# Gathering each half of an expert's list by itself, moving weight pieces out of attention's last units, and starting an expert's row preparation as soon as its rows are known

## Chip, core and metric

One core of a Trainium2 chip runs the whole program. The metric is device microseconds (us) of one execution. The engines in the profile: PE (TensorE matmul), PEld (its weight loads), DVE (VectorE), ACT (ScalarE), POOL (GpSimd), SP (SyncE, which issues most DMAs). A row with a line such as L601 names a line of the kernel before.

## What is computed

The reference chains three parts. Attention over 2 batches, 8 heads, 768 positions of 64 features: each query sees the keys less than 16 positions away and 24 block summaries (maximum of the keys, mean of the values over 32 positions). Its output, 1536 tokens of 512 features, goes through a routed layer and then a mixture:

```
# routed layer: 8 experts, each takes exactly 192 tokens
for idx in argsort(-(x @ w_gate).flatten()):   # greedy, best logit first
    tok, e = idx // 8, idx % 8
    if assigned[tok] >= 0 or counts[e] >= 192: continue
    assigned[tok] = e; counts[e] += 1
out[mask_e] = relu(x[mask_e] @ w1[e]) @ w2[e]  # 512 -> 1024 -> 512
# mixture: 4 experts, every token goes through all of them
p = domain_probs / (domain_probs.sum(-1) + 1e-9)
out = sum_e p[:, e] * (relu(x @ w1[e]) @ w2[e])
```

## The kernel before

**Numbers.** The routed layer and the mixture keep each 32-bit value as two 16-bit parts and make three matmuls for each product (`three`, L80). Each weight piece (128 x 512, 256 KB) is loaded by SP into a landing buffer (tiles `raw` and `more`, four of each after attention) and split: the high part is copied by ACT (L791), the low part is subtracted by POOL (L795), or by DVE for the first four pieces of a routed expert. `Feed` hands the pieces out in one fixed order. The first four pieces of the mixture (`POOLHI`) are split wholly by POOL.

**Attention.** 24 units of 128 tokens run in a software pipeline, `for i in range(31)`. `ORDER` and `LAST` are hand-written orders of the stages in one step. `HOOK` lists for each mixture piece handled during attention the step `i` in which it is split; the first 26 pieces (16 of mixture expert 0, 10 of expert 1) are listed, the last four at steps 27 and 28. Router steps `r0` to `r9` (`Router.first`) run in the same pipeline; their DVE lines are L520 to L545.

**Router.** `Router.phases` is a generator. Each of its 8 phases `p` fills one expert: it finds the tokens that go to it (DVE chains with small PE matmuls between, lines L622 to L706), turns the list into indices (`so`, L710; 24 to 36 matmuls into `pi`, L722), and gathers the token rows with two indirect DMAs from POOL (`gather`, L910 to L920). Each phase's 192 tokens stand in two lists of 128 and 64, since tiles hold 128 rows. A `yield r` says how long the code before it is thought to take, and the code behind it is put into the instruction stream only after about that much other work.

**The planner.** All of this is ordered while the program is written out, by a clock of the planner's own: `clock[0]` counts the matmul work put into the stream so far, in us; `clock[1]` is when the router's next step may be put in:

```
clock[1] = max(clock[:2]) + SLOW[min(known[0] + 1, len(SLOW) - 1)] * r + HOP
```

with `SLOW` 1.0 (1.3 from expert 4 on) and `HOP` 0.3. The work comes in units: of `mixture(t0, nt)`, which handles `nt` = 1, 2 or 3 tiles of 128 tokens and yields after each unit (0.66, 1.3 or 1.95 us of matmuls), and of the routed experts' jobs: one `start` (waits for the list, transposes the gathered rows on PE, splits them into `xeh` on ACT and `xel` on DVE), four `up` and four `down` (2.0 us each). `PLAN` says which experts run beside which mixture call, from when on (`at`) and how far apart (`gap`). What is left of the jobs when a mixture call ends is put in one after another (the drain, `while jobs`). `start` may be put in when `steady()` holds: its list is known, 7 us of the planner's clock have gone by (`LATE`), and its first four weight pieces have been handed out. A drained `start` does not ask `steady()`.

Of the kernel before, what the change touches and what calls it, by code (L numbers as in the profile page):

```python
# [10 lines left out]
F32 = mybir.dt.float32  # L11
F16 = mybir.dt.float16
BF = mybir.dt.bfloat16
I32 = mybir.dt.int32
# [28 lines left out]
class Feed:  # L43
# [16 lines left out]
    def next(self, free):  # L60

        self.pump()
        if self.used in self.held and self.clock[0] >= self.since[self.used] + 3.0 and free(self.used):
            self.jobs[self.used][1](self.held.pop(self.used))
            self.used += 1
            self.pump()
# [24 lines left out]
        (6, 3, [6, 7], 2.5, 4.1), (9, 3, [], 0.0, 1.0)]  # L91
WB = 5
FEED = [0.96, 0.71, 365.54]
HOOK = [10, 13, 15, 17, 18, 18, 19, 19, 20, 20, 21, 21, 22, 22, 23, 23, 24, 24, 25, 25, 26, 26, 27, 27, 28, 28]

NEXT = 4
SCHED = {"prep": [1, 1, 2, 2, 3, 4, 4, 5], "sum": 8, "v": 9, "store": 10, "spread": 11, "kq0": 4, "kq1": 7, "vn": 6}
# [362 lines left out]
class Router:  # L460
# [152 lines left out]
    def phases(self, ps, wrk, filled, place, gather, free):  # L613

        nc, m, oh, ohb, lm, E, NCH = self.nc, self.m, self.oh, self.ohb, self.lm, self.E, self.NCH
        over_chunks, over_experts = self.over_chunks, self.over_experts
        SC = NCH // 3
        four, top = self.four, self.top16
        for p in range(E):
            last = p == E - 1  # L620
            if p:
                nc.vector.tensor_tensor(lm, self.L, over_chunks(self.pen), op=OP.add)  # L622
                nc.vector.tensor_reduce(m[:, 0], lm, axis=AX.X, op=OP.max)
                if not last:

                    nc.vector.max(top[:, 0, :8], m[:, 0])
                    nc.vector.match_replace(top[:, 1, :NCH], top[:, 0, :8], m[:, 0], -3e38)
                    nc.vector.max(top[:, 0, 8:], top[:, 1, :NCH])
                    yield 1.2
                nc.vector.tensor_tensor(lm, lm, over_experts(m[:, 0]), op=OP.is_equal)  # L630
                nc.vector.tensor_tensor(lm, lm, over_chunks(self.wt), op=OP.mult)
                nc.vector.tensor_reduce(m[:, 1], lm, axis=AX.X, op=OP.max)
                nc.vector.tensor_tensor(oh, lm, over_experts(m[:, 1]), op=OP.is_equal)
                nc.vector.tensor_tensor(ohb, oh, over_experts(self.alive), op=OP.mult)
                if last:
                    yield 1.2
            new = ohb
            if p and not last:

                s4 = top[:, 0].rearrange("x (a b) -> x a b", b=4)  # L640
                yield from self.beyond(ps, wrk, s4[:, :3, 3], four[:, 5, :1])
                nc.vector.scalar_tensor_tensor(four[:, :4], self.n4.unsqueeze(1).to_broadcast([128, 4, 4]),
                                               four[:, 5, :1], s4.rearrange("x a b -> x b a"),
                                               op0=OP.is_equal, op1=OP.mult)
                cand = four[:, 6]
                nc.vector.tensor_reduce(cand, four[:, :4], axis=AX.X, op=OP.add)
                yield 1.4
                yield from self.beyond(ps, wrk, cand[:, :3], four[:, 5, 1:2])
                nc.vector.scalar_tensor_tensor(four[:, 7], self.n4, four[:, 5, 1:2], cand,
                                               op0=OP.is_equal, op1=OP.mult)  # L650
                nc.vector.tensor_reduce(four[:, 5, 2:3], four[:, 7], axis=AX.X, op=OP.add)
                yield 1.4
                pm = ps.tile([128, 128], F32, name="rt", bufs=2)
                nc.tensor.transpose(pm, four[:, 5, 2:3].to_broadcast([128, 128]), self.identf)
                yield 0.6

                nc.vector.tensor_reduce(four[:, 5, 3:4], pm, axis=AX.X, op=OP.max)
                nc.vector.tensor_scalar(m[:, 1], m[:, 0], four[:, 5, 3:4], None, op0=OP.is_gt)
                nc.vector.tensor_scalar(m[:, 2], m[:, 0], four[:, 5, 3:4], None, op0=OP.is_equal)
                new = wrk.tile([128, NCH, E], BF, name="new", bufs=1)  # L660
                nc.vector.tensor_tensor(oh, ohb, over_experts(m[:, 2]), op=OP.mult)
                nc.vector.tensor_tensor(lm, ohb, over_experts(m[:, 1]), op=OP.mult)
                above = wrk.tile([128, E], BF, name="above", bufs=1)
                nc.vector.tensor_reduce(four[:, :2].rearrange("x a b -> x (a b)"), lm.rearrange("x c e -> x e c"),
                                        axis=AX.X, op=OP.add)
                nc.vector.tensor_copy(above, four[:, :2].rearrange("x a b -> x (a b)"))
                yield 2.6
                pc = ps.tile([128, NCH, E], F32, name="rt", bufs=2)
                nc.tensor.matmul(pc, self.ones, over_chunks(above), start=True, stop=False, skip_group_check=True)
                self.ahead(pc, oh)  # L670
                yield 0.8
                nc.vector.tensor_tensor(lm, pc, over_chunks(self.remx), op=OP.is_lt)
                lead, tied = m[:, 1], m[:, 2]
                room = self.col
                nc.vector.tensor_reduce(room, lm, axis=AX.X, op=OP.min)
                nc.vector.tensor_tensor(room, room, tied, op=OP.mult)
                nc.vector.tensor_tensor(lead, lead, room, op=OP.add)
            elif not last:
                new = wrk.tile([128, NCH, E], BF, name="new", bufs=1)
                nc.vector.tensor_reduce(m[:, 1], lm, axis=AX.X, op=OP.min)  # L680
            if not last:
                nc.vector.tensor_tensor(new, ohb if p else oh, over_experts(m[:, 1]), op=OP.mult)
                yield 2.0
            pt = ps.tile([128, NCH, E], F32, name="rt", bufs=2)
            nc.tensor.matmul(pt, self.ones, new, start=True, stop=True)
            asg = self.asg if p else new
# [21 lines left out]
            so = [wrk.tile([128, SC, self.cap], F16, name="so", tag="g", bufs=GB) for _ in range(NCH // SC)]  # L708
# [5 lines left out]
                    yield 1.0  # L714
            while not free(p):
                yield 0.0
            pi = ps.tile([128, 2], F32, name="rt", bufs=2)

            for n, half, q0, s0 in sorted(((n, half, q0, s0) for half in range(2) for t, p0, n, s0 in (place(p, half),)
                                           for q0 in {0, p0}), reverse=True):  # L720
                for c in range(NCH):
                    nc.tensor.matmul(pi[q0:q0 + n, half:half + 1], so[c // SC][:, c % SC, s0:s0 + n],  # L722
                                     self.tok[:, c:c + 1], start=(c == 0 and n == 128), stop=(c == NCH - 1),
                                     skip_group_check=True)
            if p:
                yield 0.9
            gather(p, pi)
            if not p:
                nc.vector.tensor_copy(self.asg, new)
            if not last:  # L730
# [10 lines left out]
def attention_moe_mixture_kernel(  # L741
# [13 lines left out]
    nc = tc.nc  # L755
    NTOK, DM = out.shape
    E = moe_w_gate.shape[1]
    ND, _, F = moe2_w1.shape
    KD, KF = DM // 128, F // 128
    CAP = NTOK // E  # L760
    ROW = DM + ND
# [8 lines left out]
    xd = tc.dram_tile([NTOK, ROW], F32, name="xd")  # L770
# [128 lines left out]
    def place(p, half):  # L899

        t = 3 * (p // 2)
        if p % 2 == 0:
            return ((t, 0, 128, 0), (t + 1, 0, 64, 128))[half]
        return ((t + 1, 64, 64, 0), (t + 2, 0, 128, 64))[half]
# [2 lines left out]
    PD = mcst.tile([128, NST, ND], F32, name="pd")  # L907
    XG = {}

    def gather(p, pi):  # L910
        idx = []
        for half in range(2):
            t, p0, n, s0 = place(p, half)
            idx.append(wrk.tile([128, 1], I32, name="idx", bufs=4))
            nc.vector.tensor_copy(idx[half][:n], pi[:n, half:half + 1])
        for half in range(2):
            t, p0, n, s0 = place(p, half)
            nc.vector.tensor_copy(IDS[p0:p0 + n, t:t + 1], pi[p0:p0 + n, half:half + 1])
            XG[p, half] = wrk.tile([128, ROW], F32, name="xg", bufs=2)
            nc.gpsimd.indirect_dma_start(out=XG[p, half][p0:p0 + n], out_offset=None, in_=xd[:, :],  # L920
                                         in_offset=bass.IndirectOffsetOnAxis(ap=idx[half][:n, :1], axis=0))

    taken = set()
    route = router.phases(ps, wrk, filled, place, gather, lambda p: p < 1 or p - 1 in taken)
# [160 lines left out]
    for t0, nt, side, at, gap in PLAN:  # L1085
        jobs = [job for p in side for job in expert(p)]

        def begin():

            n = next((n for n, (f, _) in enumerate(jobs) if f.__name__ == "start"), 0)  # L1090
            if 0 < n <= 4 and jobs[n][1]():
                jobs.pop(n)[0]()

        now = 0.0
        for us in mixture(t0, nt):
            now += us
            spend(us)
            begin()
            while jobs and now >= at and jobs[0][1]():
                jobs.pop(0)[0]()  # L1100
                spend(2.0)
                at = max(at + gap, now)
        while jobs:
            begin()
            jobs.pop(0)[0]()
            spend(2.0)
# [27 lines left out]
```

## Time and profile before

| | us |
|---|---|
| median of 3 runs | 870.28 |
| range of the runs | 869.6 to 871.71 |
| the profiled execution, its own time | 871.12 |
| its span in the trace | 869.3 |
| PE busy | 790.5 (91% of the span) |
| DVE, ACT, POOL busy | 456.6, 291.1, 248.9 |

Between the span and the execution's own time lie 1.82 us outside the trace. Attention's pipeline ends near 136 us; from about 150 us on PE works on routed experts and mixture. A bracket at the end of a timeline row is the time for which the engine stood idle before the instruction and what ended it.

### The profile page before, as it was taken

How to read it: one execution, taken by the hardware profiler on the slowest of the kernel's cores; microseconds unless marked ns; L12 is line 12 of the kernel's file. 1: busy time of each engine (PE TensorE's matmuls, PEld its weight loads, DVE VectorE, ACT ScalarE, POOL GpSimd, SP SyncE). 2: the span in 40 equal slices, each digit the busy share in tenths (PEclk: the TensorE clock that was granted, in tenths of full speed). 3: DMA queues.
4: the chain of work that ended last, by engine and by line, in shares of the span. 5: the costliest groups of instructions: out<-in, count | busy, mean ns of one | idle time of the engine just before them, and what ended most of it. 6: DMA issues, size and time to landing. Idle time of an engine off the chain costs nothing.

```text
span 869.3 us, 17212 instructions
## 1 busy us (share of the span) xinstructions
PE 790.5 (91%) x6782; PEld 545.7 (63%) x6822; DVE 456.6 (53%) x1153; ACT 291.1 (33%) x668; POOL 248.9 (29%) x260
## 2 busy tenths in 40 slices
PE   5888974988889998989989999997999999999997
PEld 4777753866786577685556565764666664554553
DVE  6349698678765765556474566656333121321121
ACT  5788874653431222241131121412332310110110
POOL 6344553886340222160011130512412300000001
PEclk9999995999999999999999999999999999999999
DMA  9989664874412402230330121223332000000000
GB/s 199 194 207 221 176 177 141 241 221 138 128 34 80 120 16 77 69 93 2 98 104 13 33 79 55 86 77 101 94 95 61 1 1 25 13 1 1 1 1 37
DMA packets 111537, 76.27 MB, mean 88 GB/s; under 512 B 25441, under 2 KB 98273, under 8 KB 111073
## 3 DMA queue, kind: packets, MB, share of 16 engines
q1 hardware_dynamic: 109472, 68.86, 30.3%
q0 software_dynamic: 1984, 6.32, 2.4%
q8 instruction: 53, 0.87, 0.4%
q14 instruction: 28, 0.22, 0.1%
HBM read 68.77 MB, written 6.42 MB: 86 GB/s over the span
## 4 chain that ended last, share of the span: by engine, by line
PE 71%; DVE 17%; ACT 4%; DMA 4%; issue 3%; POOL 1%; SPq 0%; POOLq 0%; ACTq 0%; DVEq 0%
PE mm L80 38%; PE po L80 25%; DVE g L601 2%; DMA kq<-in_k_dram 2%; PE sc L309 1%; DVE so L710 1%; DVE hml L949 1%; DVE wp L795 1%; DVE ga L539 1%; ACT kt L263 1%; PE ta L329 1%; PE rt L595 1%; PE rt L722 1%; PE po L345 1%; ACT qt L263 1%
## 5 line engine op out<-in xcount | busy, mean ns | idle before, releaser
L948 ACT ACTIVATE hmh<-mm 128x384 f16<-128x384 f32 (+2 forms) x160 | 68.2, 426 | 308.5 <-PE mm L80 302.0
L80 PEld LDWEIGHTS <-wp 128*128 128x128 f16 (+1 forms) x1536 | 133.1, 101 | 18.6 <-issue 11.6
L949 DVE SCALAR_TENSOR_TENSOR hml<-mm,hmh 128x384 f16<-128x384 f32 (+2 forms) x160 | 75.3, 475 | 126.0 <-ACT hmh L948 125.7
L80 PEld LDWEIGHTS <-hmh 128*128 128x128 f16 x768 | 73.6, 99 | 78.9 <-issue 1.3
L795 POOL TENSOR_TENSOR wp<-raw,wp 128x512 bf16<-128x512 f32 x56 | 67.7, 1230 | 133.6 <-ACT wp L791 132.2
L601 DVE TENSOR_SCALAR g<-rt,m 128x384 bf16<-128x384 f32 x144 | 80.4, 608 | 0.7 <-PE rt L586 0.7
L80 PE MATMUL mm<-xeh,wp 128*128 128x192 f16 x512 | 74.2, 258 | 3.4 <-ACT xeh L952 3.2
L80 PE MATMUL mm<-xel,wp 128*128 128x192 f16 x256 | 66.0, 258 | 8.3 <-DVE xel L953 8.3
L1051 POOL DMA_INDIRECT out_dram<-acc,ids x12 | 12.2, 1018 | 204.0 <-DVE acc L1035 184.1
L795 POOL TENSOR_TENSOR wp<-more,wp 128x512 bf16<-128x512 f32 x40 | 45.4, 1156 | 84.2 <-ACT wp L791 84.2
L80 PE MATMUL mm<-heh,wp 128*128 128x192 f16 x512 | 69.5, 249 | 0.0
L80 PEld LDWEIGHTS <-hml 128*128 128x128 f16 x384 | 37.8, 98 | 46.4 <-issue 1.4
L80 PE MATMUL mm<-hel,wp 128*128 128x192 f16 x256 | 63.8, 249 | 0.0
L1035 DVE SCALAR_TENSOR_TENSOR acc<-po,pn,acc 128x512 f32<-128x512 f32 x36 | 25.7, 745 | 55.7 <-PE po L80 55.6
L80 PEld LDWEIGHTS <-w2k 128*128 128x128 f16 (+1 forms) x480 | 42.4, 98 | 19.2
L949 DVE SCALAR_TENSOR_TENSOR hel<-mm,heh 128x384 f16<-128x384 f32 x32 | 17.8, 558 | 63.1 <-ACT heh L948 63.0
L920 POOL DMA_INDIRECT xg<-xd,idx x16 | 16.1, 1003 | 122.0 <-DVE m L731 99.2
L948 ACT ACTIVATE heh<-mm 128x384 f16<-128x384 f32 x32 | 15.7, 491 | 88.6 <-PE mm L80 88.6
L80 PEld LDWEIGHTS <-w23dt.float 128*128 128x128 f16 x320 | 29.5, 98 | 14.4 <-issue 1.3
L80 PEld LDWEIGHTS <-w21dt.float 128*128 128x128 f16 x320 | 30.0, 99 | 12.6
L791 ACT ACTIVATE wp<-more 128x512 f16<-128x512 f32 x64 | 37.0, 622 | 1.3 <-DMA more<-in_moe_w_dram 1.1
L80 PE MATMUL po<-w23dt.float,hml 128*128 128x512 f16 x96 | 36.9, 384 | 0.6 <-issue 0.2
(255 smaller groups left out, 1926.5 us busy)
## 6 DMA issues: line engine op xcount, KB each, us to landing
raw<-in_moe_w_dram SPq DMA_DIRECT2D x110, 256.0 KB, 3.5
more<-in_moe_w_dram SPq DMA_DIRECT2D x82, 256.0 KB
vb<-in_v_dram SPq DMA_DIRECT2D x16, 240.0 KB, 6.0
kq<-in_k_dram SPq DMA_DIRECT2D x8, 384.0 KB, 6.5
kq<-in_q_dram SPq DMA_DIRECT2D x8, 384.0 KB, 5.9
vn<-in_v_dram SPq DMA_DIRECT2D x4, 768.0 KB, 9.9
xd<-x SPq DMA_DIRECT2D x48, 64.0 KB, 4.0
vb<-vsum_d SPq DMA_DIRECT2D x4, 292.5 KB
```

What stands on the lines that cost most here:

```text
L80: nc.tensor.matmul(o, a[i], b[j], start=first and n == 0, stop=last and n == 2, skip_group_check=True)
L263: nc.scalar.activation(o[:, :, :, :, r], pt[r * 64:r * 64 + 64].rearrange("x j (c i) -> x c i j", i=R), AF.Copy, scale=scale)
L309: nc.tensor.matmul(sc[:, t, p], QT[Q][:, p, 2 * ch + t], KT[Q][:, p, 2 * ch + t], start=False, stop=True, skip_group_check=True)
L329: nc.tensor.transpose(pt[:KC, p], AE[u][:, p], identf)
L601: nc.vector.tensor_scalar(g[:, c - c0], row, m[:, 0, c:c + 1], None, op0=OP.is_le)
L791: nc.scalar.activation(hi, r, AF.Copy)
L795: (eng or nc.gpsimd).tensor_tensor(lo, r, hi, op=OP.subtract)
L920: nc.gpsimd.indirect_dma_start(out=XG[p, half][p0:p0 + n], out_offset=None, in_=xd[:, :], in_offset=bass.IndirectOffsetOnAxis(ap=idx[half] ...
L948: nc.scalar.activation(h[0], p, AF.Relu)
L949: nc.vector.scalar_tensor_tensor(h[1], p, 0.0, h[0], op0=OP.max, op1=OP.subtract)
L1035: nc.vector.scalar_tensor_tensor(acc[i], po[i], s, acc[i], op0=OP.mult, op1=OP.add)
L1051: nc.gpsimd.indirect_dma_start(out=out[:, :], out_offset=bass.IndirectOffsetOnAxis(ap=IDS[:, t0 + i:t0 + i + 1], axis=0), in_=acc[i], in_o ...
```

## The change

1. `HOOK` has 24 entries in place of 26. Steps 12 and 16 get one piece more, steps 27 and 28 lose two each. Pieces 8 and 9 of mixture expert 1 are now among the four handled between attention and the routed experts, and four instead of two of that expert's pieces come behind the 16 of the first routed expert.
2. Four of the router's `yield`s are longer.
3. The matmuls for an expert's list go into one PSUM tile for each half, and `gather` handles one half. In phase 0 the first half's gather is put in ahead of the second half's matmuls; in the other phases both gathers follow the matmuls, the longer half first.
4. `begin()` also puts in a `start` that is the first of the jobs (`n == 0`), without waiting for `at`, and then the next job is held back 2.5 us of the planner's clock.

```diff
-HOOK = [10, 13, 15, 17, 18, 18, 19, 19, 20, 20, 21, 21, 22, 22, 23, 23, 24, 24, 25, 25, 26, 26, 27, 27, 28, 28]
+HOOK = [10, 12, 13, 15, 16, 17, 18, 18, 19, 19, 20, 20, 21, 21, 22, 22, 23, 23, 24, 24, 25, 25, 26, 26]
...
                 if last:
-                    yield 1.2
+                    yield 2.6
...
                 nc.vector.tensor_reduce(four[:, 5, 2:3], four[:, 7], axis=AX.X, op=OP.add)
-                yield 1.4
+                yield 2.0
                 pm = ps.tile([128, 128], F32, name="rt", bufs=2)
...
                 nc.vector.tensor_copy(above, four[:, :2].rearrange("x a b -> x (a b)"))
-                yield 2.6
+                yield 3.6
                 pc = ps.tile([128, NCH, E], F32, name="rt", bufs=2)
...
                 nc.vector.tensor_tensor(new, ohb if p else oh, over_experts(m[:, 1]), op=OP.mult)
-                yield 2.0
+                yield 2.8
             pt = ps.tile([128, NCH, E], F32, name="rt", bufs=2)
...
-            pi = ps.tile([128, 2], F32, name="rt", bufs=2)
...
+            todo = []
+            for half in sorted(range(2), key=lambda half: -place(p, half)[2]):
+                t, p0, n, s0 = place(p, half)
+                pi = ps.tile([128, 1], F32, name="rt", bufs=2)
+                for q0 in sorted({0, p0}, reverse=True):
+                    for c in range(NCH):
+                        nc.tensor.matmul(pi[q0:q0 + n], so[c // SC][:, c % SC, s0:s0 + n],
+                                         self.tok[:, c:c + 1], start=(c == 0), stop=(c == NCH - 1),
+                                         skip_group_check=True)
+                todo.append((half, pi))
+                if not p:
+                    gather(p, *todo.pop())
             if p:
                 yield 0.9
-            gather(p, pi)
+            for half, pi in todo:
+                gather(p, half, pi)
...
+    def gather(p, half, pi):
+        t, p0, n, s0 = place(p, half)
+        idx = wrk.tile([128, 1], I32, name="idx", bufs=4)
+        nc.vector.tensor_copy(idx[:n], pi[:n])
+        XG[p, half] = wrk.tile([128, ROW], F32, name="xg", bufs=2)
+        nc.gpsimd.indirect_dma_start(out=XG[p, half][p0:p0 + n], out_offset=None, in_=xd[:, :],
+                                     in_offset=bass.IndirectOffsetOnAxis(ap=idx[:n, :1], axis=0))
+        nc.vector.tensor_copy(IDS[p0:p0 + n, t:t + 1], pi[p0:p0 + n])
...
-            n = next((n for n, (f, _) in enumerate(jobs) if f.__name__ == "start"), 0)
-            if 0 < n <= 4 and jobs[n][1]():
+            n = next((n for n, (f, _) in enumerate(jobs) if f.__name__ == "start"), 9)
+            if n <= 4 and jobs[n][1]():
                 jobs.pop(n)[0]()
+                return n == 0
...
-            begin()
+            if begin():
+                at = max(at, now + 2.5)
```

## Rows read from the trace of the kernel before

**Rows 1.** The page's chain of work that ended last, shares by engine.
```profile
PE 71%; DVE 17%; ACT 4%; DMA 4%; issue 3%; POOL 1%; SPq 0%; POOLq 0%; ACTq 0%; DVEq 0%
```

**Rows 2.** Windows: length, busy us (count) of PE, PEld, DVE, ACT, POOL; clock, DMA, GB/s.
```profile
157.00:625.00 468.00, 433.94 (x3995) 309.30 (x4020) 291.58 (x763) 136.42 (x304) 150.68 (x133) 0.98 0.31 88
...
180.00:200.00 20.00, 14.72 (x158) 10.06 (x157) 16.66 (x28) 8.79 (x22) 17.13 (x16) 0.91 0.67 203
```

**Rows 3.** Waits of PE, 157 to 625 us: total us, times, longest.
```profile
PE mm L80 <- DVE xel L953: 7.9, 6, 3.0
PE mm L80 <- ACT xeh L952: 2.7, 6, 0.8
```

**Rows 4.** Timeline of PE: start us, duration, instruction, idle before and its releaser.
```profile
192.05 0.32 PE L654 MATMUL rt<-identf,four 128*128 128x128 f32 x1 [3.62 <-DVE four L651]
200.28 0.22 PE L669 MATMUL rt<-above,ones 128*128 128x96 bf16 x1 [1.72 <-DVE above L666]
216.21 1.00 PE L722 MATMUL rt<-tok,so 128*128 128x1 f16 x28 [0.72 <-DVE so L710]
230.40 0.32 PE L80 MATMUL mm<-xel,wp 128*128 128x192 f16 x1 [1.53 <-DVE xel L953]
334.90 0.20 PE L685 MATMUL rt<-new,ones 128*128 128x96 bf16 x1 [1.16 <-DVE new L682]
347.14 1.00 PE L722 MATMUL rt<-tok,so 128*128 128x1 f16 x28 [1.23 <-DVE so L710]
373.68 0.32 PE L80 MATMUL mm<-xel,wp 128*128 128x192 f16 x1 [3.04 <-DVE xel L953]
444.93 0.32 PE L80 MATMUL mm<-xel,wp 128*128 128x192 f16 x1 [1.58 <-DVE xel L953]
566.67 0.20 PE L669 MATMUL rt<-above,ones 128*128 128x96 bf16 x1 [2.40 <-DVE above L666]
596.94 0.22 PE L685 MATMUL rt<-ohb,ones 128*128 128x96 bf16 x1 [3.30 <-DVE ohb L634]
```

**Rows 5.** Windows of two stretches behind such waits.
```profile
444.00:450.00 6.00, 5.08 (x39) 4.33 (x39) 2.88 (x8) 1.42 (x3) 0.33 (x1) 0.72 0.04 11
566.00:572.00 6.00, 5.33 (x53) 5.16 (x53) 2.09 (x7) 0.33 (x1) 1.70 (x2) 0.72 0.00 0
```

**Rows 6.** Timelines of DVE and POOL in attention's last steps.
```profile
128.00 0.23 DVE L522 SCALAR_TENSOR_TENSOR lm<-L,m,wt 128x8 f32<-128x8 f32 x1
128.45 0.23 DVE L526 TENSOR_SCALAR oh<-lm,m 128x8 bf16<-128x8 f32 x1
...
131.20 0.77 DVE L522 SCALAR_TENSOR_TENSOR lm<-L,m,wt 128x8 f32<-128x8 f32 x1
...
132.20 0.89 DVE L526 TENSOR_SCALAR oh<-lm,m 128x8 bf16<-128x8 f32 x1
...
130.79 2.27 POOL L795 TENSOR_TENSOR w21dt.bfloat<-raw,w21dt.float 128x512 bf16<-128x512 f32 x2 [3.92 <-ACT w21dt.float L791]
```

**Rows 7.** Timelines of DVE and POOL at the first gather.
```profile
143.47 0.22 DVE L915 CAST idx<-rt 128x1 int32<-128x1 f32 x2 [1.09 <-PE rt L722]
...
149.91 0.69 DVE L953 SCALAR_TENSOR_TENSOR xel<-mm,xeh 128x512 f16<-128x512 f32 x1 [0.35 <-ACT xeh L952]
...
144.50 1.18 POOL L920 DMA_INDIRECT xg<-xd,idx  x1 [7.24 <-ACT wp L791]
```

**Rows 8.** Later gathers: tile `xg`'s landing times, POOL's timeline; ACT's and DVE's behind a `down`.
```profile
DMA to landing us min/median/max: 2.8/3.4/4.9
...
219.63 0.91 POOL L920 DMA_INDIRECT xg<-xd,idx  x1 [6.88 <-DVE idx L915]
220.84 0.97 POOL L920 DMA_INDIRECT xg<-xd,idx  x1 [0.30 <-DVE hml L949]
...
366.08 0.33 ACT L952 ACTIVATE y1h<-mm 128x192 f16<-128x192 f32 x1 [8.86 <-PE mm L80]
...
366.44 0.36 DVE L953 SCALAR_TENSOR_TENSOR y1l<-mm,y1h 128x192 f16<-128x192 f32 x1 [2.81 <-ACT y1h L952]
```

More of the change, by code (lines that the diff above doesn't have):

```diff
@@ L716, in phases @@
                 yield 0.0
-            pi = ps.tile([128, 2], F32, name="rt", bufs=2)
[L719 to L724, printed above, removed]
+            todo = []
[10 more added lines that the diff above has]
+                    gather(p, *todo.pop())
             if p:
                 yield 0.9
-            gather(p, pi)
+            for half, pi in todo:
+                gather(p, half, pi)
             if not p:
@@ L908, in attention_moe_mixture_kernel @@
     XG = {}
[L910 to L921, printed above, removed]
+    def gather(p, half, pi):
[6 more added lines that the diff above has]
+        nc.vector.tensor_copy(IDS[p0:p0 + n, t:t + 1], pi[p0:p0 + n])
     taken = set()
```

## The prediction

> **What bounds the kernel now.** I read the chain of waits first. PE holds 71% of it and DVE 17% [rows 1]: behind attention the time is matmul work plus the moments in which PE waits. None of the matmuls of that work is removed or added, so the change can only move those moments and attention's end. The windows give their size: from 157 to 625 us PE was busy 433.94 of 468 us, so it idled 34 us, at a mean clock of 0.98 [rows 2]. Next the waits of PE in that stretch. Two kinds are to be seen. In the first, a new expert's first `up` matmuls wait for its rows' two parts: 7.9 us for `xel` and 2.7 for `xeh`, six times each [rows 3], 10.6 us. In the second, one of the router's small matmuls stands in PE's queue and its DVE operand is late: 3.62, 1.72, 0.72, 1.16, 1.23, 2.40 and 3.30 us in the timeline [rows 4]. PE works in order, so all matmuls behind such a one wait too. Third, the clock behind some of these waits: from 444 to 450 and from 566 to 572 us the mean granted clock is 0.72 [rows 5]. With levels of 1.2 and 2.4 GHz that loses 0.28 x 6 = 1.7 us each. Such dips stand behind six of the waits (192.05, 230.40, 347.14, 373.68, 444.93, 566.67); the 3.30 us at 596.94 has none.
>
> I make the sum against the profiled execution, 871.12 us, which is 0.84 above the median.
>
> **Attention's end.** Four pieces stood in steps 27 and 28. Around the first low parts that POOL makes of them (2.27 us from 130.79), DVE's L522 takes 0.77 us against 0.23 before it, and L526 0.89 against 0.23 [rows 6]: 0.54 + 0.66 = 1.2 us of DVE, whose chain ends attention. With no piece there I count that as removed. Steps 12 and 16 get one piece each, where PE, ACT and DVE share the chain; between nothing and the same 1.2 us I take 0.4, since there the load is spread over more engines. Net -0.8, bounds -1.2 to 0.
>
> **First gather.** `idx` of both halves is copied at 143.47, after DVE waited 1.09 us for the matmuls of both; POOL starts the first gather at 144.50 [rows 7]. With one half done first, its copies fall into that wait: DVE is through 0.4 us earlier (two index casts and two copies, half of them moved). The gather itself starts up to 1.4 us earlier, but before `xel` at 149.91 DVE had stood idle only 0.35 us, so what came next was DVE, not the rows. I take -0.4; bounds -1.4 and 0.
>
> **Longer yields.** What matters is how many units of work lie between a DVE step and the small matmul that reads it. A step of 1.4 + 0.3 (HOP) fills with three units of 0.66, 1.98 us; 2.0 + 0.3 with four, 2.64. Phase 1 at 192.05: 0.66 of 3.62 goes. In the same way, at 200.28, 2.9 against 3.9 gives 5 or 7 units of 0.65, so 1.3 of 1.72 goes. At 334.90 (2.3 against 3.1, two or three units of 1.3) all 1.16. At 566.67 the factor 1.3 makes 3.68 or 4.98, two or three units of 1.95; less a job's 2.0 for a unit, 1.83 of 2.40. At 596.94, 1.86 or 3.68, one or two units: 1.94 of 3.30. Sum 6.9 [rows 4], and the dip behind 566.67, 1.7 [rows 5]: -8.6. Below this: nothing, if DVE's delay is carried on to the next step.
>
> **Starts put in early.** The planner, followed unit by unit, puts two units between `start` and the first `up` for experts 2, 4 and 6, where before the `up` followed at once. `xel` waits of experts 1, 3 and 4 are 1.53, 3.04 and 1.58 [rows 4]; what is left of 7.9 is 1.75 for experts 2, 5 and 6, 0.58 each, and with 2.7 / 6 = 0.45 for `xeh` [rows 3] a plain start costs 1.03. So experts 2 and 6 save 1.03 each and expert 4 saves 2.03 and its dip of 1.7 [rows 5]: -5.8. Expert 1's start stays in a drain, but the router is a step behind and no comparison of its search stands ahead of `xel` on DVE; I take its wait from 1.98 to 1.03, and half of the dip: -1.8, bounds -2.7 to +1. Expert 5's stays at 1.03.
>
> **Phase 3's list.** At 347.14 the index matmuls waited 1.23 us for `so` [rows 4] with one unit of 1.3 between; now this lies in the drain with jobs of 2.0 between. The wait and its dip go: -2.9, bounds -2.9 to 0.
>
> **The price: expert 3's start.** Each router phase is now up to 2.4 us longer (0.6 + 1.0 + 0.8), and whole units round it up. Phase 3's gather moves from 163.2 to 177.5 on the planner's clock, and expert 3's `start`, which is drained and asks nothing, stands right there; before it stood 16 us behind. So nothing covers the gather. Behind the last `down` of expert 2: 0.33 + 0.36 us for its parts, on the queue of which the index casts stand [rows 8], about 0.4 for the casts and POOL's reaction, 1.21 until POOL issues the second gather (219.63 to 220.84), which is the half that `start` reads first, and 3.4 to its landing [rows 8]: 5.7, and a plain start's 1.03, 6.7 us of idle PE. It replaces 3.04 + 0.45 = 3.5; the dip stays. +3.2, bounds +1.5 (landing 2.8, less queue) to +8 (landing 4.9, and DVE as crowded as at 373.68).
>
> **Given back elsewhere.** In phase 1 two `so` steps now have 1.31 us between where 1.95 stood, behind which 0.72 was waited [rows 4]: +1.3, and a dip of 1.7, as the 1.23 at 347.14 has one. And the two pieces that left attention are split again about 200 us, where POOL is busy 17.13 of 20 us and PE idles most [rows 2]; two more low parts of 1.14 us (half of 2.27 [rows 6]) stretch DVE by up to 2.3 us, some of it in front of PE: +1.0. Together +4.0, bounds +1 to +6.
>
> On that last term the Trainium skill (SBUF — State Buffer, Who interferes with whom) speaks against the change: VectorE and GpSimd share a port pair as a lock, and whichever starts first keeps it for the whole instruction while the other is blocked. The rows of attention's end agree in kind: DVE lost 1.2 us of the 2.27 that POOL worked. By the rule taken to its full length the term would be 2.3 and not 1.0, and the sum 1.3 us higher; the split of DVE's waiting that the rows show is what I use.
>
> **Sum.** -0.8 - 0.4 - 8.6 - 5.8 - 1.8 - 2.9 + 3.2 + 4.0 = -13.1: 858.0 for the profiled execution, 857.2 for the median. I say 857.
>
> **Rivals.** (a) *The idle goes, the clock does not come back.* Dips stand behind waits of 1.23 as of 3.62 us, and 3.30 had none [rows 4], so which waits bring one is not plain. With the dips of 1.7, 1.7, 0.85 and 1.7 kept, 6.0 is lost again: 863. (b) *The wait only moves.* DVE's router chain is as long as before, and POOL still stretches it; if each longer gap is used up by DVE being further behind at the next small matmul, the yields' 8.6 and phase 3's 2.9 are gone: 857.2 + 11.5 = 868.7, no change that can be told. For it: 3.62 us for a single operand at 192.05. Against it: at most router matmuls PE did not wait at all. (c) *The other side: rows that come too late at drained starts.* Expert 1's gather to start shrinks too, from 7.2 to 5.85 us of planner's clock, about what the chain above needs (5.7). If landings take 4.9 us [rows 8] and DVE is crowded as at 373.68 (3.04), each idles about 10.5: 4.9 in place of 3.4, and 3.0 in place of 0.58 more, with their own dips. Expert 3 then costs 4 more than counted, and expert 1 gives back its 1.8 and loses 8.5 and 0.9. That is 15 us: 872. It is slower than before from about 16 us on, which a third such start, expert 5's, would bring (+9): 881.
>
> **How the numbers follow.** A measurement of this kernel can tell about 0.3%, 2.6 us, from no change. Chances: the forecast, 847 to 862, 0.52; (a), 860 to 866, 0.22; (b), and other losses that leave about the old time, 0.15; (c) 0.11. (a) and the forecast lie below 867.7, (b) between 867.7 and 872.9 in most of its cases, (c) on either side of 872.9, mostly above. Faster 0.76, same 0.13, slower 0.11. The range reaches from 847, where the bounds of the gains come out (0.4 more at attention's end, 1.0 at the gather, 0.9 at expert 1, 1.7 at expert 3, 3 given back less, together 7 and the uneven rest 3), to 869, which takes in (b).
>
> **What would show it.** Right: the rows of L654, L669, L685 with idle times of about 3.0, 0.4 or less, 0.6, 1.4 and none; no waits for `xel` at experts 2, 4 and 6; a window of 0.72 at neither expert 4's first `up` nor phase 6's L669; one wait of 6 to 7 us for `xg` and `xeh` at expert 3; attention's last DVE steps about 1 us earlier; from 157 us on PE idle of some 24 in place of 34 us. Wrong: idle at L672's and L722's neighbours grown by what left the others (b), dips of the same number as before (a), or PE standing at `xg` at expert 1 (c).

## The result and the profile after

The changed kernel takes 855.75 us (median of 4 runs, 853.86 to 856.93) against 869.94 for the kernel before beside it; ratio 0.9837, 95% interval 0.9806 to 0.9867. The forecast was 857. The profiled execution took 856.93 us, 14.2 less than the one before; its span is 855.2 us, 14.1 less.

The page's chain of waits, which answers to [rows 1]: DVE's share fell from 17 to 12%, that of DMA rose from 4 to 6.

```profile
PE 73%; DVE 12%; DMA 6%; ACT 4%; issue 3%; POOL 2%; SPq 0%; POOLq 0%; DVEq 0%; ACTq 0%
```

The windows of [rows 2]. PE idles 23.4 us of 468, where it idled 34.1 (32.4 in a second execution of the kernel before, whose trace holds 4036 matmuls in this window and not 3995, so a part of the 34.1 may be missing records). The mean clock is 0.98 as before.

```profile
157.00:625.00 468.00, 444.56 (x4020) 311.24 (x4019) 289.63 (x755) 136.14 (x302) 143.89 (x126) 0.98 0.30 86
180.00:200.00 20.00, 16.25 (x171) 10.50 (x169) 16.90 (x29) 8.55 (x21) 17.80 (x17) 0.91 0.70 209
```

PE's waits from 157 to 625 us, total, times, longest [rows 3]. The router's L654, L669 and L685, five of the waits in [rows 4], are not among them any more. New at the top is PE waiting for gathered rows, and second the mixture's own matmuls waiting for `hml` (the low part of relu, on DVE; 7.1 us, where 0.5 us stood before).

```profile
PE mm L972 <- DMA xg<-xd,idx: 8.4, 2, 7.6
PE mm L80 <- DVE hml L951: 7.1, 6, 3.8
PE mm L80 <- DVE xel L955: 2.9, 3, 2.1
PE mm L80 <- ACT xeh L954: 2.6, 3, 1.2
PE rt L595 <- DVE g L601: 1.3, 4, 0.4
```

PE's timeline at those waits. The first two stand where L654 and L669 of phase 1 waited 3.62 and 1.72; then expert 1's start, expert 2's, expert 3's (7.64, the price), and expert 5's.

```profile
192.06 0.22 PE L80 MATMUL mm<-y0h,w21dt.float 128*128 128x128 f16 x1 [3.75 <-DVE hml L951]
205.37 0.22 PE L80 MATMUL mm<-y0h,w2k 128*128 128x128 f16 x1 [1.09 <-DVE hml L951]
...
227.25 1.05 PE L972 MATMUL mm<-identf,xg 64*128 64x64 f32 x8 [0.80 <-DMA xg<-xd,idx]
228.98 0.24 PE L80 MATMUL mm<-xeh,wp 128*128 128x192 f16 x1 [0.69 <-ACT xeh L954]
229.70 0.24 PE L80 MATMUL mm<-xel,wp 128*128 128x192 f16 x1 [0.48 <-DVE xel L955]
...
300.57 1.04 PE L972 MATMUL mm<-identf,xg 128*128 128x128 f32 x8 [0.35 <-DVE hml L951]
302.28 0.27 PE L80 MATMUL mm<-y0h,w2k 128*128 128x256 f16 x1 [0.67 <-DVE hml L951]
...
367.17 1.74 PE L972 MATMUL mm<-identf,xg 64*128 64x64 f32 x8 [7.64 <-DMA xg<-xd,idx]
369.59 0.32 PE L80 MATMUL mm<-xeh,wp 128*128 128x192 f16 x1 [0.68 <-ACT xeh L954]
370.32 0.32 PE L80 MATMUL mm<-xel,wp 128*128 128x192 f16 x1 [0.41 <-DVE xel L955]
...
541.17 0.24 PE L80 MATMUL mm<-xeh,wp 128*128 128x192 f16 x1 [1.23 <-ACT xeh L954]
543.46 0.24 PE L80 MATMUL mm<-xel,wp 128*128 128x192 f16 x1 [2.05 <-DVE xel L955]
```

What is late at 192.05 and 192.06 is one small DVE operation, the same in both kernels. L649 handles 4 elements a partition and takes 0.22 us at its shortest; here it takes 4.13 us before and 4.16 after. `hml` is the next but one behind it on DVE. Beside it POOL splits weights without a break, and L649 ends when that row of splits ends: at 191.71 against 191.69 us before, at 191.62 against 191.60 after, and within 0.03 us in all fourteen traces below. The operations just ahead of it, L609 to L611, ran in the same stretch and took 0.16 to 0.18 us. The first four lines are of before, the others of the changed kernel.

```profile
187.39 0.16 DVE L611 TENSOR_REDUCE four<-four 128x1 f32<-128x3 f32 x1
187.58 4.13 DVE L649 SCALAR_TENSOR_TENSOR four<-n,four 128x4 f32<-128x4 f32 x1
188.31 1.16 POOL L795 TENSOR_TENSOR w2k<-more,w2v 128x512 bf16<-128x512 f32 x1
189.42 2.27 POOL L795 TENSOR_TENSOR w23dt.bfloat<-more,w23dt.float 128x512 bf16<-128x512 f32 x2
...
187.46 4.16 DVE L649 SCALAR_TENSOR_TENSOR four<-n,four 128x4 f32<-128x4 f32 x1
191.65 0.16 DVE L651 TENSOR_REDUCE four<-four 128x1 f32<-128x4 f32 x1
191.72 0.68 DVE L951 SCALAR_TENSOR_TENSOR hml<-mm,hmh 128x128 f16<-128x128 f32 x3
...
185.98 4.51 POOL L801 TENSOR_TENSOR w2k<-raw,w2v 128x512 bf16<-128x512 f32 x4
190.43 1.17 POOL L801 TENSOR_TENSOR w2k<-more,w2v 128x512 bf16<-128x512 f32 x1
```

Expert 3's start on POOL, in the order in which the prediction followed it. The second gather is issued 1.29 us behind the first, and its rows arrive when PE goes on at 367.17, 5.25 us after issue; the median counted with was 3.4 [rows 8]. In the window around it the mean clock is 0.53 for 11 us.

```profile
360.63 0.98 POOL L921 DMA_INDIRECT xg<-xd,idx  x1 [3.56 <-DVE idx L919]
361.92 0.97 POOL L921 DMA_INDIRECT xg<-xd,idx  x1 [0.30 <-DVE remx L742]
...
363.00:374.00 11.00, 5.74 (x34) 4.87 (x35) 4.23 (x12) 1.50 (x3) 1.15 (x1) 0.53 0.55 148
```

DVE at attention's end [rows 6]. L522 and L526 take 0.23 us, as forecast, with no piece beside them. But L534 and L539 now stand 0.53 and 0.29 us waiting for ACT and PE, so L539 starts 1.86 us behind L522 where it started 2.06 us behind it before (133.26 - 131.20; first line, of before).

```profile
133.26 1.14 DVE L539 TENSOR_SCALAR ga<-rows,m 128x768 bf16<-128x768 f32 x2
...
131.98 0.23 DVE L522 SCALAR_TENSOR_TENSOR lm<-L,m,wt 128x8 f32<-128x8 f32 x1
...
132.44 0.23 DVE L526 TENSOR_SCALAR oh<-lm,m 128x8 bf16<-128x8 f32 x1
133.20 0.35 DVE L534 SCALAR_TENSOR_TENSOR ge<-rows,m,before 128x128 bf16<-128x128 f32 x1 [0.53 <-ACT rows L530]
133.84 1.15 DVE L539 TENSOR_SCALAR ga<-rows,m 128x768 bf16<-128x768 f32 x2 [0.29 <-PE cnt L564]
```

**A finer measure.** Attention's end moves between executions; what follows it much less. So I also compare, in each trace, the time from the first matmul of expert 0's `up` (L80, `mm<-xeh`; 150.33 us before, 150.00 after) to the end of the span. All times in us; "L710 starts" is the first comparison that builds the index matrices, the mark of attention's end. e1 to e4 were taken on one chip and e5 to e10, c1 and c2 on another; each ratio is against the kernel before on the same chip.

| trace | L710 starts | first up | first up to end | ratio of the runs (95%) |
|---|---|---|---|---|
| before | 139.7 | 150.33 | 719.0 | |
| before, again (c1) | 138.9 | 149.45 | 717.2 | |
| changed | 140.0 | 150.00 | 705.2 | 0.9837 (0.9806 to 0.9867) |
| changed, again (c2) | 140.2 | 150.11 | 705.5 | |
| e1, yields alone | 142.5 | 153.10 | 705.5 | 0.9896 (0.9868 to 0.9924) |
| e2, starts alone | 140.0 | 150.57 | 707.2 | 0.9883 (0.9863 to 0.9903) |
| e3, HOOK alone | 137.8 | 148.44 | 721.4 | 1.0042 (1.0015 to 1.0069) |
| e4, gather alone | 137.5 | 147.48 | 719.9 | 1.0008 (0.9982 to 1.0034) |
| e5, changed, old yields in phases 1 to 3 | 139.2 | 149.47 | 704.8 | 0.9867 (0.9813 to 0.9921) |
| e6, changed, old HOOK | 136.3 | 146.31 | 700.4 | 0.9833 (0.9793 to 0.9874) |
| e7, both of these | 137.7 | 147.62 | 704.7 | 0.9807 (0.9762 to 0.9853) |
| e8, e7 with starts ahead of the weights | 136.6 | 146.62 | 695.1 | 0.9726 (0.9679 to 0.9774) |
| e9, e8 with L669's longer yield in phase 1 | 137.8 | 147.78 | 696.9 | 0.9719 (0.9642 to 0.9797) |
| e10, e8 with all longer yields | 142.9 | 152.74 | 706.5 | 0.9854 (0.9772 to 0.9935) |

### The profile page after: what moved, and what is told of

It reads as the page before. It is cut to its first block, busy times and chain, and to the rows that moved or that the text cites. A ratio compares the mean times of both kernels' runs of the same rounds, so it can differ in the third digit from the quotient of the medians.

```text
span 855.2 us, 17243 instructions
## 1 busy us (share of the span) xinstructions
PE 787.2 (92%) x6822; PEld 542.9 (63%) x6822; DVE 456.9 (53%) x1153; ACT 291.8 (34%) x668; POOL 250.3 (29%) x260
## 4 chain that ended last, share of the span: by engine, by line
PE 73%; DVE 12%; DMA 6%; ACT 4%; issue 3%; POOL 2%; SPq 0%; POOLq 0%; DVEq 0%; ACTq 0%
PE mm L80 40%; PE po L80 27%; DVE g L601 2%; DMA xd<-x 2%; DMA kq<-in_k_dram 1%; DMA xg<-xd,idx 1%; ACT kt L263 1%; PE rt L595 1%; POOL w20dt.bfloat L801 1%; PE rt L724 1%; ACT qt L263 1%; DVE hml L951 1%; DVE so L710 1%; DVE ga L539 1%; DMA vsum_d<-vs 1%
## 5 line engine op out<-in xcount | busy, mean ns | idle before, releaser
L80 PEld LDWEIGHTS <-wp 128*128 128x128 f16 (+1 forms) x1536 | 132.0, 101 | 14.6 <-issue 7.2
L80 PEld LDWEIGHTS <-hmh 128*128 128x128 f16 x768 | 73.3, 98 | 79.0 <-issue 0.8
L801 POOL TENSOR_TENSOR wp<-raw,wp 128x512 bf16<-128x512 f32 x54 | 65.8, 1238 | 132.6 <-ACT wp L797 132.5
L601 DVE TENSOR_SCALAR g<-rt,m 128x384 bf16<-128x384 f32 x144 | 80.5, 609 | 0.0
L80 PE MATMUL mm<-xeh,wp 128*128 128x192 f16 x512 | 75.3, 260 | 3.1 <-ACT xeh L954 3.1
L801 POOL TENSOR_TENSOR wp<-more,wp 128x512 bf16<-128x512 f32 x42 | 48.1, 1166 | 74.4 <-ACT wp L797 74.2
L80 PE MATMUL mm<-xel,wp 128*128 128x192 f16 x256 | 66.5, 260 | 3.4 <-DVE xel L955 3.4
L80 PE MATMUL mm<-heh,wp 128*128 128x192 f16 x512 | 68.0, 246 | 0.0
L80 PEld LDWEIGHTS <-hml 128*128 128x128 f16 x384 | 37.7, 98 | 45.8 <-issue 0.8
L80 PE MATMUL mm<-hel,wp 128*128 128x192 f16 x256 | 63.0, 246 | 0.2 <-DVE hel L951 0.2
L80 PEld LDWEIGHTS <-w2k 128*128 128x128 f16 (+1 forms) x480 | 42.5, 98 | 21.1 <-issue 1.9
L80 PEld LDWEIGHTS <-w21dt.float 128*128 128x128 f16 x320 | 29.4, 98 | 16.8 <-issue 3.9
L80 PEld LDWEIGHTS <-w23dt.float 128*128 128x128 f16 x320 | 29.6, 98 | 14.0 <-issue 1.3
L797 ACT ACTIVATE wp<-raw 128x512 f16<-128x512 f32 x64 | 37.1, 621 | 1.7 <-DMA raw<-in_moe_w_dram 1.7
```

The lines of the kernel that those rows point to most:

```text
L80: nc.tensor.matmul(o, a[i], b[j], start=first and n == 0, stop=last and n == 2, skip_group_check=True)
L601: nc.vector.tensor_scalar(g[:, c - c0], row, m[:, 0, c:c + 1], None, op0=OP.is_le)
L797: nc.scalar.activation(hi, r, AF.Copy)
L801: (eng or nc.gpsimd).tensor_tensor(lo, r, hi, op=OP.subtract)
```

## The experiments

**Each part alone, on the kernel before.** e1 has the four `yield`s of the diff, e2 the new `begin()` with its `at = max(at, now + 2.5)`, e3 the new `HOOK`, e4 the two hunks of `pi` and `gather`; nothing else differs.

> The four longer yields alone, on the kernel before. The theory (each part by its own step of the sum): the waits of PE at L654, L669 and L685 go (about 9 us with a clock dip), but expert 3's start comes to stand 2 us of planner's clock behind its gather instead of 16, which costs about 5 us there; ratio 0.993 to 0.998. The rival (the wait only moves: DVE is as late at the next step): 0.998 to 1.003, with the same PE idle from 155 to 625 us as before, about 34 us.

Measured: 0.9896, a gain of 1.0% where the theory gave 0.2 to 0.7%, and 705.5 us from the first up. No wait of 0.5 us is left at L669 and L685, and PE idles 23.8 us from 155 to 625 us, so the rival falls as an account of the whole. At L654 it holds: the wait is now one of 3.75 us for `hml`. Expert 3's start waits 2.62 us for `xg` and 1.05 for DVE, as expected in kind, but with its parts that is 4.4 us where 3.8 stood, not 5 more. Expert 5's start, which the theory did not name, waits 3.8 us where 0.9 stood.

> The new begin() alone. The theory: two units of the mixture now lie between start and first up of experts 2, 4 and 6, so their waits for xel and xeh go and so does the clock dip at expert 4: about -6 us, 0.993 (0.990 to 0.996). The rival (the starts' gain hangs on the longer yields, since without them DVE's search comparisons still stand ahead of xel): 0.998 or more.

Measured: 0.9883, and 707.2 us. Expert 4's waits are gone, expert 6's are down to 0.87 us for `hml`, as the theory says. It is more than the theory gave: the waits at 334.90, 347.14, 566.67 and 596.94 of [rows 4], which the prediction gave to the yields and to phase 3's list, are gone here too, with the old yields. That the jobs now fall elsewhere among the router's steps is the likely reason; no run tests it. The rival falls.

> HOOK alone. The theory after seeing the changed kernel: DVE's work at attention's end is shorter, but the steps there then wait for ACT and PE, and the step's earlier units lose as much: attention's end within 0.7 us of before, 0.998 to 1.002. The rival, as the prediction had it: 0.8 us earlier at attention's end, 1 us lost again at 200 us, also no difference in the time, but the index comparisons (L710) would begin about 0.8 us earlier.

Measured: 1.0042, slower by 0.4%, with the interval above 1. L710 starts at 137.8 in this trace, but that says little: over the fourteen traces above it starts at 139.0 on average in the ten with the old list (136.3 to 142.9) and at 139.3 in the four with the new one (137.8 to 140.2). The difference from both traces of the kernel before is behind the first up: 721.4 us against 719.0 and 717.2. The index matmuls of phase 1 wait longer, 1.58 us where 0.72 was [rows 4], and a dip stands behind that wait:

```profile
215.18 0.97 PE L722 MATMUL rt<-tok,so 128*128 128x1 f16 x27 [1.58 <-DVE so L710]
...
216.00:221.00 5.00, 5.00 (x65) 4.99 (x63) 1.94 (x14) 1.21 (x5) 1.51 (x2) 0.66 0.33 88
```

That the part costs time is shown by the runs. Where it costs it is seen in this one trace: 0.9 us of the wait and 1.7 us of the dip, and single dips come and go between executions (last section). Its benefit at attention's end is not shown; the rival's earlier end is not borne out over the traces.

> The gather by halves alone. The theory: the first gather starts about 0.4 us earlier, DVE is the engine that the first up waits for, so the first up begins 0.3 to 0.7 us earlier and nothing else changes: 0.9985 to 1.0005. The rival (POOL is held by something else than the index cast): no earlier start of the first gather.

Measured: 1.0008, no difference. From the start of L710 to the first up are 10.0 us (147.48 - 137.48) against 10.65 before (150.33 - 139.68): 0.65 us earlier, near the upper end of the theory. This repeats best of all: 10.6 to 10.65 us in the five traces with the old gather, 9.9 to 10.3 in the nine with the new one. The theory's reason does not hold; PE's wait ahead of the first up is for the rows (First gather, below).

**Undoing parts of the changed kernel.** e5 keeps the old yields in phases 1 to 3, e6 the old `HOOK`, e7 both.

```diff
-                yield 2.0
+                yield 2.0 if p > 3 else 1.4
                 pm = ps.tile([128, 128], F32, name="rt", bufs=2)
...
-                yield 3.6
+                yield 3.6 if p > 3 else 2.6
                 pc = ps.tile([128, NCH, E], F32, name="rt", bufs=2)
...
-                yield 2.8
+                yield 2.8 if p > 3 else 2.0
             pt = ps.tile([128, NCH, E], F32, name="rt", bufs=2)
```

> The changed kernel, with the old yields in phases 1 to 3 and the new ones from phase 4 on (and in the last). Expert 3's gather then stands 9.9 us of planner's clock ahead of its start again instead of directly before it. The theory: the 7.6 us wait for xg goes, and the time from the first up to the end falls from 705.2 to about 699 us (696 to 702); phases 1 and 3 get waits of about 1 us back. The rival (the longer yields earn their gain in phases 1 to 3, and the wait for xg only takes the place of other waits): 705 us or more from the first up to the end.

Measured: 704.8 us, no gain; the theory falls and the rival holds. The wait for `xg` is gone, but expert 3's start still waits 1.24 + 2.04 us for its parts, and phase 1's waits are back:

```profile
199.31 0.22 PE L669 MATMUL rt<-above,ones 128*128 128x96 bf16 x1 [1.91 <-DVE above L666]
216.31 0.84 PE L724 MATMUL rt<-tok,so 128*128 128x1 f16 x23 [1.58 <-DVE so L710]
```

> The changed kernel with the old HOOK. The theory: the two pieces behind attention cost about 2.4 us around 200 us (as HOOK alone showed) and buy nothing measurable at attention's end, so from the first up to the end 702 to 704 us against 705.2. The rival (with the other parts in, the pieces fit where PE no longer waits): 705 us, no difference.

Measured: 700.4 us from the first up, 5 us less than the changed kernel. Expert 1's start waits as long as in the changed kernel (0.76 + 0.69 + 0.48 = 1.93 us against 1.97). What is gone is the wait of 0.77 us for `hml` at 215.58, 0.8 us of the wait for `xg` (6.87) and the dip behind expert 1's start, 1.7 us: three stretches run at the lower clock instead of four. The direction is the theory's, in one trace; the ratios of the runs (0.9833 against 0.9837) don't tell the two apart.

> Both of these: old HOOK, and the old yields in phases 1 to 3. The theory: both savings, 695 to 700 us from the first up to the end, ratio to the kernel before 0.974 to 0.982. The rival (each saving only moves a wait): 703 us or more.

Measured: 704.7 us, 0.9807. The two savings do not add; the rival holds.

**A version that beats both.** e8 takes e7 and lets a start go ahead without its weights.

```diff
             need(p)
-            ready(p, 3)
+            if p == 0:
+                ready(p, 3)
...
-            return known[0] >= p and clock[0] >= when[p] + LATE and feed.used > feed.at["p", p, 3]
+            return known[0] >= p and clock[0] >= when[p] + LATE
```

> As the kernel with old HOOK and late yields, and start no longer asks for the expert's first four weight pieces (except for expert 0), so that the starts of experts 3 and 5 go ahead of the last downs of the expert before (2.0 us and 11.8 us of work between start and first up, where none stood). The theory: their waits for xeh and xel, about 3 us each with a clock dip of 1.7 to 3 us each, go: 6 to 9 us less from the first up to the end than without this, 688 to 693 us. The rival (the first up waits for the weights instead, which are split only after start): at most 2 us less.

Measured: 695.1 us, 9.6 less than e7; ratio to the kernel before 0.9726. Expert 5's start has no wait of 0.5 us left, expert 3's are down to 1.4 us, and the clock stays at 1.00 there:

```profile
360.91 0.24 PE L80 MATMUL mm<-xeh,wp 128*128 128x192 f16 x1 [0.78 <-DVE xel L955]
361.73 0.24 PE L80 MATMUL mm<-xel,wp 128*128 128x192 f16 x1 [0.58 <-DVE xel L955]
...
360.00:364.00 4.00, 2.63 (x35) 2.39 (x34) 3.94 (x9) 1.54 (x4) 1.16 (x1) 1.00 0.45 133
```

The runs agree: the medians are 844.91 and 853.24 us, beside each other. The waits that went at experts 3 and 5 are 4.5 us and the dip at expert 3 is 1.7. The rest is not all the edit's: the dips behind L669 and behind expert 1's start are gone too, the latter behind waits as long as in e7 (0.69 + 1.52 us).

The level expected, 688 to 693, was built on e7's, which was itself too low; the difference to e7 is a little above the 6 to 9 us given.

e9 changes `3.6 if p > 3` to `3.6 if p > 3 or p == 1`; e10 is the changed kernel with the old `HOOK` and e8's two edits.

> As the kernel whose starts go ahead of the weights (e8), with the longer yield before L669 (3.6 in place of 2.6) in phase 1 too. The theory: of the wait of 1.9 us at L669 some 1.3 us goes, 693 to 695 us from the first up to the end against 695.1. The rival (DVE is late by as much at the next matmul): 695 us or more, with a wait for hml in its place.

Measured: 696.9 us, 0.9719: the rival. The wait at L669 falls by 1.4 us and one for `hml` appears right behind it:

```profile
197.84 0.22 PE L669 MATMUL rt<-above,ones 128*128 128x96 bf16 x1 [0.54 <-DVE above L666]
203.75 0.22 PE L80 MATMUL mm<-y0h,w2k 128*128 128x128 f16 x1 [1.98 <-DVE hml L951]
```

> As e8, with the longer yields in all phases, so that expert 3's gather stands directly before its start again. The theory: the wait for xg of 7 us and its long stretch at 1.2 GHz come back at expert 3, against which the waits of phases 1 and 3 (about 5 us) go: 694 to 699 us from the first up to the end. The rival (the wait for xg is not worth more than the waits that the yields remove): 692 us or less.

Measured: 706.5 us, 11.4 more than e8 and above the theory's range. The wait for `xg` is back (5.46 us, and ten us at the lower clock), and it brings a second cost that e8's rival had named: expert 3's weight pieces are handed out only behind its start, so its first up waits 1.21 us for a piece's high part on ACT, and its matmuls then wait for POOL six times, 0.86 to 0.89 us each.

```profile
378.92 0.34 PE L80 MATMUL mm<-xeh,wp 128*128 128x192 f16 x2 [0.89 <-POOL wp L801]
```

**The same kernels again.**

> The kernel before once more, for the spread of the measure used here. The theory: attention's end moves by one to three us from one execution to another, and the time from the first up of expert 0 to the end repeats within 1 us: 718 to 720. The rival: that time spreads as much as attention's end, by 3 us or more, and differences of 2 to 5 us between single traces mean nothing.

> The changed kernel once more, for the same question. The theory: 704 to 706 us from the first up to the end, with the wait of 7 to 8 us for xg at expert 3 again. The rival: another 3 us or more off 705.2.

Measured: 717.2 and 705.5 us, with the wait for `xg` at 7.04. The theory holds for the changed kernel; for the one before the two differ by 1.8 us, more than the theory's 1. Differences of 2 to 3 us between single traces are at the edge of this. Those of 9 and more are far outside it; the 5 us of e6 contain a dip and are not confirmed by its runs.

## Why the prediction was right, step by step

**The whole.** From the first up to the end 13.8 us went (11.9 forecast), ahead of it 0.3 in the two profiled executions (1.2 forecast). That waits of PE bound the kernel agrees with this: idle PE from 157 to 625 us fell by 10.6 us (444.56 - 433.94), or by 9.0 against the second execution of the kernel before (435.57).

**That the sum came within 1.5 us is in part luck.** Errors on both sides nearly cancel. Less was saved than forecast at attention's end (0.8), at experts 1 and 2 (2.8) and at expert 5, which lost 2.4 us and a dip, and the price at expert 3 was 1.7 higher. Against this stand the 3.0 us of phase 1's index matmuls that were not given back and 3.7 us of router waits that nobody had counted. The mechanism of the largest gains, PE no longer waiting for late DVE operands at the router's matmuls and at starts with work behind them, is what the traces show.

**Attention's end, -0.8: wrong.** The 1.2 us of DVE went as forecast. The step that failed is "DVE, whose chain ends attention": DVE then waited for ACT and PE, and no earlier end shows in the fourteen traces.

**First gather, -0.4: right in size**, 0.65 by e4; **wrong in its reason.** That "what came next was DVE, not the rows" does not hold for PE. Its transposes waited 1.77 us for the gathered rows before and 1.21 after, and the first up followed 2.2 us behind their start in both. POOL starts the first gather 4.82 us behind L710's start before and 4.17 after, the same 0.65 us, and 1.0 to 1.1 us behind the start of the index cast in both, whatever its bracket names. The 1.4 us that the prediction allowed for did not come. The first line is of before.

```profile
148.13 1.73 PE L970 MATMUL mm<-identf,xg 128*128 128x128 f32 x8 [1.77 <-DMA xg<-xd,idx]
...
147.77 1.76 PE L972 MATMUL mm<-identf,xg 128*128 128x128 f32 x8 [1.21 <-DMA xg<-xd,idx]
...
143.07 0.16 DVE L919 CAST idx<-rt 128x1 int32<-128x1 f32 x1 [0.36 <-PE rt L724]
...
144.18 1.18 POOL L921 DMA_INDIRECT xg<-xd,idx  x1 [16.52 <-DMA raw<-in_moe_w_dram]
```

**Longer yields, -6.9 of idle: right in sum, not in place.** At 200.28, 334.90, 566.67 and 596.94 of [rows 4] all 8.6 us went, where 6.2 was forecast; three of these four waits go by the early starts alone as well (e2), so they are not the yields' alone. Two of the terms were not worked out well: by the rule of whole units 3.9 us fill with six units of 0.65, not seven, which gives 0.65 at 200.28 and not 1.3; and how 1.83 at 566.67 follows from a unit of 1.95 and a job of 2.0 is not plain. At 192.05 nothing went: 3.62 became 3.75, now as a wait for `hml`, and 1.09 more stands at 205.37. That is rival (b), and it holds for this one step: the late DVE operation, L649, also stands in the queue ahead of the relu whose buffer the next mixture matmuls need, so more work in between did not help. The prediction's "3.62 us for a single operand" is L649 held beside POOL's weight splits. No run here moves those splits away, so what that would save is not tested.

**Starts put in early, -5.8 and -1.8: half right.** Experts 4 and 6 lost their whole waits. Expert 2 has 0.35 + 0.67 us for `hml` in place of its 0.9. Expert 1 waits 0.80 + 0.69 + 0.48 = 1.97, no gain, 0.8 of it for `xg`, where rival (c) had looked. "Expert 5's stays at 1.03" failed: 1.23 + 2.05. There the router's L601 (1.14 us from 541.02) and a weight split now stand on DVE just ahead of `xel`, as they did at expert 3 before (370.75).

**Phase 3's list, -2.9: right;** no wait there, no dip.

**The price at expert 3, +3.2: right in mechanism, mis-sized.** Idle is 7.64 + 0.68 + 0.41 = 8.7 us, not 6.7, because the landing took 5.25 us and not 3.4. What it replaced was 3.04 + 0.80 = 3.8, not 3.5 (0.45 was a mean over six experts), so the net price in idle is 4.9. And "the dip stays" was too kind: some ten us ran at the lower level.

**Given back, +4.0: mis-sized in its parts.** The `so` steps of phase 1 did not wait more (0.77, now for `hml`), so of the 3.0 for them nothing came. The pieces split later cost 3.3 us (e3, against the mean of the two traces before) to 5 us (e6 against the changed kernel) by single traces, where 1.0 was taken; by the runs they cost 0.4%, 3.7 us, in e3 and nothing in e6, so the size stays open. The rule of the Trainium skill weighed there (SBUF — State Buffer, Who interferes with whom), taken to its full length, gave an estimate of 2.3, nearer to the single traces than my 1.0. The trace agrees with it in kind: L649 lasted 4.16 us beside POOL, and 0.22 elsewhere. That the two later pieces made this longer is not shown, since L649 took 4.13 us before.

**Not counted at all:** smaller waits of the router (1.24, 0.82, 0.75, 0.49 and 0.41 us at L586, 3.7 together), none of which is in the changed kernel's trace behind 150 us.

**The clock.** The forecast had 4.3 us come back. The loss by the clock's rows from 155 to 640 us is 10.2 us before and 10.4 in the changed kernel, and 8.5 and 12.2 in their second executions. Three dips are gone (behind 347.14, 444.93 and 566.67), one is new behind expert 5's start, and the one at expert 3 is long. Some of the loss falls on idle time; weighted with PE's busy share of each us it is 9.3 and 7.9 us, and 7.8 and 9.3 in the second executions, so nothing came back that repeats. Rival (a) was right in this.

**The parts do not add.** Yields alone save 12.6 us and starts alone 10.8 against the mean of the two traces before (718.1). The changed kernel saves 12.8 with both. Of the 10.6 that are missing, HOOK explains some 3 to 5 by single traces (e3: 3.3; e6: 5). For the rest two things are seen. Both parts alone remove the same waits of phases 3, 6 and 7 (1.16, 1.23, 2.40 and 3.30 us of [rows 4], 8.1 together), which can be saved only once. And with both, expert 3's start waits 8.7 us, where it waits 4.4 in e1 and 3.3 in e2. e5 shows that the collision cannot be had back by the old yields: they cost as much in phases 1 to 3. How the rest divides is not settled.

## What to carry to other kernels

Where a planner's order decides, take the waits of the bounding engine one by one, and ask of each what stands behind the late operation in its queue: a longer gap helps the reader of the operand only if nothing else behind it is needed as soon (192.05). Look at how long the late operation itself takes and what runs beside it: the longest single wait of [rows 4], 3.62 us, was a DVE operation of 0.22 us that lasted 4.13 us beside POOL, and neither gaps nor early starts touched it. When steps are put further apart, follow the last one of the chain to its own deadline; here that deadline cost 8.7 us. Spacing the chain differently only moved the waits (e5, e9); letting the preparation go ahead of what it does not need (e8) removed expert 5's and more than half of expert 3's. Compare traces from a mark behind the part that varies.

## What was not expected of the hardware

A wait of the same length does not always bring the clock down. Before (first two rows) and in its second execution (last two), PE waited the same 1.23 and 1.58 us at the same instructions; behind them the granted clock was 0.57 and 0.66 in the one and 1.00 in the other.

```profile
349.00:353.00 4.00, 3.78 (x14) 1.72 (x13) 2.48 (x17) 0.38 (x1) 1.71 (x2) 0.57 0.11 28
444.00:449.00 5.00, 4.08 (x32) 3.73 (x32) 1.99 (x6) 0.42 (x2) 0.00 (x0) 0.66 0.04 13
```

```profile
345.00:349.00 4.00, 4.00 (x49) 2.82 (x47) 1.32 (x10) 0.38 (x1) 0.52 (x1) 1.00 0.24 70
441.00:446.00 5.00, 3.88 (x41) 3.17 (x41) 3.44 (x10) 1.53 (x3) 0.70 (x1) 1.00 0.08 24
```

It goes the other way too: the wait of 3.30 us at 596.94 had no dip behind it, and the same wait of 3.31 us had one in the second execution. The waits themselves repeat to 0.1 us in most places, the dips don't: six before, four in its repetition (10.2 and 8.5 us lost). And attention's end moves by 6.6 us (136.3 to 142.9) over the ten traces with the old `HOOK`. The seven runs of the kernel before beside c1 spread by 11.5 us (865.74 to 877.22); how much of that is attention's end no trace shows.
